# q of the later batches turned by DMA as k is, and the last output rows in three column pieces

## The chip, the core and the metric

The kernel runs on one NeuronCore of a Trainium2 chip. A core has five engines, each with an instruction list of its own that it takes in order: PE (TensorE, matrix multiply), DVE (VectorE), ACT (ScalarE), POOL (GpSimd) and SP (SyncE, which here only issues DMAs). They meet at semaphores. Data lies in HBM, in SBUF (128 partitions) and in PSUM, where TensorE writes its results, in eight banks of 512 float32 columns. The metric is the device time of one execution in microseconds (us).

## The reference

For each of 8 batches and 8 heads, with 576 positions of 64 values, it computes causal attention over a sliding window of 64 positions; the result, 4608 rows (8 x 576) of 512 values (8 heads x 64), goes through a two-layer network with a hidden width of 2048.

```python
scores = scale * np.matmul(q, k.transpose(0, 1, 3, 2))
rel = pos[:, None] - pos[None, :]
mask = (rel >= 0) & (rel < window)          # window = 64
attn = softmax(np.where(mask, scores, -1e9))
x = np.matmul(attn, v)                      # then (B, S, H, D) -> (B*S, H*D)
h = x @ w_in                                # 512 -> 2048
out = (h * sigmoid(h)) @ w_out              # 2048 -> 512
```

## The kernel before, in words

**The order is planned in the program.** `Plan` (L15) holds operations in classes, each class a queue with a rank, and plays them through once with a cost per engine; whichever ready operation has the lowest rank goes next on a free engine. What comes out is one fixed list for each engine. The first layer and second layer matmuls (class `moe`) have rank 99, so on TensorE they fill every place that attention leaves. Scores (class `s`) may only go in while second-layer matmuls are due, or when the next first layer lacks its input (`scores_may_run`, L439).

**Attention.** Heads are taken in pairs: four pairs `pj` for each batch, and three groups `g` of 192 positions. For a pair the kernel needs, in bfloat16, k with the 128 values of two heads on the partitions and positions along the columns (`kt`), and q in the same way but padded with zeros (`qbd`): head 0 sits on partitions 0 to 63 in one half, head 1 on partitions 64 to 127 in the other, so that one matmul gives the scores of both heads. `kt`, `qbd` and `vv` (v) have two buffers, used by batches in turn. Then come the exponential on ACT (`expo`, L334), the mask on DVE (`masking`, L337), the values matmul (`values`, L340) and the division on DVE (`inverse`, `normal_rows`). From batch 3 on the result is written to `oxs` and a DMA on SP transposes it into `bridge` (`turn_o`, L391), the network's input.

**How q and k get their layout.** By the older way, used for batches 0 and 1 and for every q, SP (POOL in batches 1 and 2) loads two heads in float32 into one of eight `nat` buffers (`load_qk`, L227), ACT or DVE casts it into `natb` (`cast`, L270), TensorE turns it in six transposing matmuls of 96 columns into PSUM (`turn`, L279), and ACT or DVE lifts it from there in two halves into `qbd` (`lift_q`, L287), or for k in one into `kt`. By the newer way, used for k from batch 2 on (`NXK`), POOL loads each head's rows and casts them on the way into one of two `kb` buffers (`load_k_rows`, L239, four loads for two pairs), and one transposing DMA on SP writes two pairs into `kt` (`turn_k`, L245). `add_batch_qk` (L452) enters all this in the plan. A load into `nat` or `kb` waits until the buffer's last reader is done, and from batch 3 on until v of the batch before has landed.

**The network.** The rows are cut into 9 tiles of 512 (`add_tile`, L564). The first layer makes 16 blocks of 128 hidden units in 64 matmuls and ACT applies the activation (`silu`); the second layer takes, for each of four blocks of 128 rows, 16 matmuls of 512 columns into one bank (`second_layer`, L416). DVE or ACT copies the bank into one of four `ot` buffers (`copy_out`), and SP stores it (`store`, L425), 128 rows of 512 values. Tile 8, the last, ends the program.

Of the kernel before, what the change touches and what calls it, by code (L numbers as in the profile page):

```python
# [9 lines left out]
BF16 = mybir.dt.bfloat16  # L10
# [98 lines left out]
def kernel(ctx, tc, q, k, v, w_in, w_out, out):  # L109
    nc = tc.nc  # L110
    B, H, S, D = q.shape
    d_model, d_ff = w_in.shape
# [3 lines left out]
    NM = 6  # L116
    NR = S // NM
    NG = 3
    NDC = d_model // 128
    NFT = d_ff // 128  # L120
    TT = 512
    NTT = B * S // TT
    TB = TT // 64
    NK = 2
    NN, NNB, NE, NOB, NOT, NGT = 8, 8, 14, 6, 4, NFT + 3
    PARTS = {0: [(0, 192), (192, 384), (384, TT)], 1: [(0, 256), (256, TT)]}
    NXK, NXO = 2, 3
    NKB, NOX = 2, 2
    scale = 1.0 / float(D) ** 0.5


# [2 lines left out]
    keep = ctx.enter_context(tc.tile_pool(name="keep", bufs=1))  # L134
# [13 lines left out]
    es = [keep.tile([128, 3, 2, 64], BF16, name=f"e{i}") for i in range(NE)]  # L148
    rcs = [keep.tile([128, 3, 2], FP32, name=f"rc{i}") for i in range(4)]
    obs = [keep.tile([128, 3, 128], BF16, name=f"ob{i}") for i in range(NOB)]  # L150
    kbs = [keep.tile([NR, 2, NM, 128], BF16, name=f"kb{i}") for i in range(NKB)]
    oxs = [keep.tile([128, 3, NP, 128], BF16, name=f"ox{i}") for i in range(NOX)]
    gts = [keep.tile([128, TT], BF16, name=f"g{i}") for i in range(NGT)]
    ots = [keep.tile([128, d_model], FP32, name=f"ot{i}") for i in range(NOT)]
# [6 lines left out]
    p = Plan(  # L161
        {"at": range(4), "mp": range(4, 8), "all": range(8)},
        rank=dict(one=-9, dma=-1, ld0=-1, ld1=-1, st=-2, xo=-1.5, xk=-1.4, silu=-3, out=-2, pv=0, ot=0, s=1, moe=99, warm=200, turn=2,
                  norm=0, inverse=0, bridge=0, exp=1, mask=1, lift=2, shift=2, cast=4, late=5, clear=9),
        rank0=dict(cast=-6, lift=-5, shift=-4.5, exp=-4, mask=-4, inverse=-3.5, norm=-3, bridge=-3.2),
    )
    copies = {"ACT": nc.scalar.copy, "DVE": nc.vector.tensor_copy, "POOL": nc.gpsimd.tensor_copy}
# [68 lines left out]
            in_=k[b, 2 * pj + hh].rearrange("(p m) d -> p m d", m=NM),  # L236
        )

    def load_k_rows(w, b, pj, hh):  # L239
        nc.gpsimd.dma_start(  # L240
            out=kbs[w][:, pj % 2, :, 64 * hh:64 * hh + 64],
            in_=k[b, 2 * pj + hh].rearrange("(m p) d -> p m d", p=NR),
        )

    def turn_k(w, b, pp):  # L245
        nc.sync.dma_start_transpose(
            out=kt[b % NK][:, 64 + 2 * pp * S:64 + 2 * (pp + 1) * S].rearrange("x (m p) -> x m p", m=2 * NM),
            in_=kbs[w].rearrange("p j m x -> p (j m x)"))

    def load_v(e, b, part):  # L250
        g0, g1 = part * 9, part * 9 + 9
# [161 lines left out]
    def silu(bank, gt, lo, hi):  # L413
        nc.scalar.activation(out=gts[gt][:, lo:hi], in_=banks[bank["bank"]][:, lo:hi], func=ACTF.Silu)  # L414

    def second_layer(bank, gt, m, f):  # L416
        nc.tensor.matmul(  # L417
            banks[bank["bank"]], lhsT=gts[gt][:, m * 128:(m + 1) * 128], rhs=w_out_sb[:, f, :],
            start=(f == 0), stop=(f == NFT - 1),
        )  # L420

    def copy_out(e, bank, ot):
        copies[e](out=ots[ot], in_=banks[bank["bank"]])  # L423

    def store(ot, j, m):  # L425
        r0 = j * TT + m * 128
        nc.sync.dma_start(out=out[r0:r0 + 128, :], in_=ots[ot])


    win, wout = [], []  # L430
# [16 lines left out]
        return rest > 6  # L447
    scores_may_run.i = 0

    n_nat, n_kb, kb_free = [0, 0], [0], {}  # L450

    def add_batch_qk(b):  # L452
        pool = "at" if b else "all"
        k_rows, k_busy = [], []
        for pj in range(NP):
            kq_done[(b, pj)] = []
            busy = s_last.get((b - NK, pj), []) + ([c_k[b % NK]] if b < NK else [])
            for kk in range(2):
                if b >= NXK and kk:
                    w = n_kb[0] // 2 % NKB  # L460
                    n_kb[0] += 1
                    k_rows += [p.add("dma", {"POOL": 0.72}, lambda _, w=w, pj=pj, hh=hh: load_k_rows(w, b, pj, hh),
                                     kb_free.get(w, []) + (v_landed[b - 1] if b > 2 else []), dma=0.6) for hh in range(2)]
                    k_busy += busy
                    if pj % 2:
                        xk = p.add("xk", {"SP": 1.4}, lambda _, w=w, pj=pj: turn_k(w, b, pj // 2), k_rows + k_busy, dma=2.9)
                        kb_free[w] = [xk]
                        for i in (pj - 1, pj):
                            kq_done[(b, i)].append(xk)
                        k_rows, k_busy = [], []  # L470
# [24 lines left out]
                tu["until"] = li  # L495
                kq_done[(b, pj)] += li
# [67 lines left out]
    def add_tile(j):  # L564
        gt = {}
        parts = PARTS.get(j, [(0, TT)])
        for ft in range(NFT):
            gt[ft] = (n_gt[0] % NGT, [])
            n_gt[0] += 1
        left = NFT * NDC * len(parts)  # L570
        for lo, hi in parts:
            have = o_done[:NP * ((j * TT + hi + 191) // 192)]
            for ft in range(NFT):
                g, si = gt[ft]
                bank = None
# [11 lines left out]
        order = [(m, f) for m in range(4) for f in range(NFT)]  # L587
        if j == 0:
            order = [(m, f) for f in range(NFT) for m in range(4)]
        bank, uses = {}, {}  # L590
        for i, (m, f) in enumerate(order):
            g = gt[f][0]
            op = p.add("moe", {"PE": 0.2165}, None, gt[f][1] + [wout[f // 2]], lat=0.1, pool=None if f else "mp")
            bank.setdefault(m, op)
            op["fn"] = lambda _, bank=bank[m], g=g, m=m, f=f: second_layer(bank, g, m, f)
            moe.append((op, 2, len(order) - i))
            uses.setdefault(g, []).append(op)
            if f == NFT - 1:
                ot = n_ot[0] % NOT
                n_ot[0] += 1  # L600
                cp = p.add("out", {"DVE": 0.7, "ACT": 0.62}, lambda e, bank=bank[m], ot=ot: copy_out(e, bank, ot),
                           [op, free_ot.get(ot)])
                bank[m]["until"] = [cp]
                free_ot[ot] = p.add("st", {"SP": 0.45}, lambda _, ot=ot, m=m: store(ot, j, m), [cp], dma=0.75)
        free_gt.update(uses)


# [59 lines left out]
```

## Time and profile before

| | |
|---|---|
| median of 8 runs | 326.32 us (325.48 to 327.17) |
| the profiled execution | 325.48 us, of which 323.4 us are its span |
| granted TensorE clock | full speed in all 40 slices |
| transposing DMAs on SP | 12 into `kt`, 15 into `bridge` |
| row loads of k on POOL | 48, of 72 KB each, 5.5 us from issue to landing |
| loads of q on SP | 24, of 288 KB each, 5.4 us from issue to landing |

From the page, in 40 equal slices of some 8 us each, tenths of busy time:

```profile
PE   3999989999999999999999999999999999999995
...
DVE  7895988875788948899789778800000000000000
ACT  4798775898787986788887875274156126416611
POOL 8967958581706603822713000000000000000000
...
DMA  8999999999999929999999111310110020020011
```

Attention, with all loads of q, k and v, goes on until about 210 us, between the matmuls of tiles 0 to 4; after that four tiles of the network alone are left. A group's line in the profile gives line, engine, operation, output<-input and count, then the busy time, the mean duration of one, and the idle time of the engine just before.

### The profile page before, as it was taken

What the parts mean: (1) busy time and instruction counts of PE and PEld (TensorE: products, weight loads), DVE (VectorE), ACT (ScalarE), POOL (GpSimd) and SP (SyncE); (2) the same over time, 40 slices, a digit from 0 to 9 for tenths busy, and PEclk for the clock granted to TensorE, in tenths of its full rate; (3) what the DMA queues carried; (4) which work ended last, traced back from release to release, by engine and by line L of the source; (5) the groups of instructions that cost most, each with busy time, mean ns of one, the idle gap of its engine ahead of it and who ended that gap; (6) DMA issues with size and microseconds to landing.
All of it is one profiled execution on the core that took longest, in us unless ns stands there. A gap on an engine that the chain in (4) does not pass through costs nothing.

```text
span 323.4 us, 6343 instructions
## 1 busy us (share of the span) xinstructions
PE 310.5 (96%) x2349; PEld 178.4 (55%) x2349; DVE 171.7 (53%) x480; ACT 207.8 (64%) x420; POOL 96.6 (30%) x126
## 2 busy tenths in 40 slices
PE   3999989999999999999999999999999999999995
PEld 1778865578565556655565555544444444444442
DVE  7895988875788948899789778800000000000000
ACT  4798775898787986788887875274156126416611
POOL 8967958581706603822713000000000000000000
PEclk9999999999999999999999999999999999999999
DMA  8999999999999929999999111310110020020011
GB/s 199 171 190 277 183 214 216 140 267 161 192 215 158 216 33 152 167 259 138 235 184 205 28 49 37 112 59 0 65 67 0 32 97 3 2 96 34 0 65 65
DMA packets 112350, 40.29 MB, mean 125 GB/s; under 512 B 95808, under 2 KB 106944, under 8 KB 112320
## 3 DMA queue, kind: packets, MB, share of 16 engines
q0 software_dynamic: 75520, 16.29, 59.7%
q1 hardware_dynamic: 36800, 23.60, 29.7%
q8 instruction: 18, 0.29, 0.4%
q14 instruction: 12, 0.10, 0.1%
HBM read 36.70 MB, written 9.44 MB: 143 GB/s over the span
## 4 chain that ended last, share of the span: by engine, by line
PE 86%; DVE 8%; DMA 2%; issue 1%; SPq 1%; ACT 1%; ACTq 0%
PE mp L417 38%; PE mp L408 34%; PE at L343 5%; PE at L317 4%; DVE qbd L289 4%; DMA nat<-in_q_dram 2%; PE at L282 2%; DVE natb L271 2%; DVE vv L303 1%; DVE vv L305 1%; DVE kt L295 1%; PE at L399 1%; SPq L228 1%; PE at L388 0%; PE at L609 0%
## 5 line engine op out<-in xcount | busy, mean ns | idle before, releaser
L417 PE MATMUL mp<-w_out_sb,g 128*128 128x512 bf16 x576 | 146.9, 379 | 0.0
L408 PE MATMUL mp<-bridge,w_in_sb 128*128 128x512 bf16 (+3 forms) x768 | 133.2, 326 | 0.9 <-ACT g L414 0.9
L414 ACT ACTIVATE g<-mp 128x512 bf16<-128x512 f32 (+3 forms) x192 | 90.5, 491 | 25.4 <-PE mp L408 23.6
L408 PEld LDWEIGHTS <-w_in_sb 128*128 128x128 bf16 x768 | 69.0, 98 | 50.7 <-issue 1.4
L417 PEld LDWEIGHTS <-g 128*128 128x128 bf16 x576 | 52.5, 98 | 42.0
L423 ACT COPY ot<-mp 128x512 f32<-128x512 f32 x24 | 14.0, 585 | 55.1 <-PE mp L417 55.0
L335 ACT ACTIVATE e<-at 128x384 bf16<-128x384 f32 x88 | 38.4, 498 | 12.0 <-PE at L317 10.4
L252 POOL DMA_DIRECT2D vv<-in_v_dram x32 | 32.4, 1021 | 41.7 <-DVE e L338 14.9
L372 DVE TENSOR_TENSOR ox<-at,rc 64x192 bf16<-64x192 f32 x120 | 42.5, 354 | 2.7
L240 POOL DMA_DIRECT2D kb<-in_k_dram x48 | 35.8, 754 | 25.8 <-DMA kt<-kb 22.1
L343 PEld LDWEIGHTS <-e 128*128 128x128 bf16 x288 | 22.6, 96 | 15.1 <-DVE e L338 2.5
L338 DVE TENSOR_TENSOR e<-e,mask 128x384 bf16<-128x384 bf16 x84 | 25.8, 350 | 8.3 <-ACT e L335 7.7
L343 PE MATMUL at<-vv,e 128*128 128x130 bf16 x276 | 29.9, 219 | 0.0
L289 DVE COPY qbd<-at 64x576 bf16<-64x576 bf16 x29 | 21.8, 752 | 6.0 <-PE mp L408 2.8
L289 ACT COPY qbd<-at 64x576 bf16<-64x576 bf16 x33 | 20.8, 630 | 6.4 <-DVE qbd L289 3.9
L317 PE MATMUL at<-qbd,kt 128*128 128x128 bf16 x252 | 24.3, 219 | 0.4 <-DVE qbd L289 0.4
L317 PEld LDWEIGHTS <-kt 128*128 128x128 bf16 x252 | 18.6, 97 | 10.2 <-issue 1.4
L282 PE MATMUL at<-ident,natb 96*128 96x96 bf16 x228 | 16.2, 210 | 7.2 <-ACT natb L271 5.5
L349 DVE RECIPROCAL rc<-at 128x6 f32<-128x6 f32 x92 | 17.1, 192 | 10.3 <-PE at L343 7.3
L282 PEld LDWEIGHTS <-natb 96*128 96x128 bf16 x240 | 13.7, 100 | 13.0 <-ACT natb L271 5.7
L271 ACT CAST natb<-nat 96x768 bf16<-96x768 f32 x20 | 16.2, 834 | 2.3 <-DMA nat<-in_q_dram 1.9
L355 DVE TENSOR_TENSOR ob<-at,rc 64x192 bf16<-64x192 f32 x48 | 16.8, 350 | 0.9
(67 smaller groups left out, 159.5 us busy)
## 6 DMA issues: line engine op xcount, KB each, us to landing
out_dram<-ot SPq DMA_DIRECT2D x36, 256.0 KB, 2.1
nat<-in_q_dram SPq DMA_DIRECT2D x24, 288.0 KB, 5.4
vv<-in_v_dram POOLq DMA_DIRECT2D x32, 144.0 KB, 5.6
kb<-in_k_dram POOLq DMA_DIRECT2D x48, 72.0 KB, 5.5
nat<-in_q_dram POOLq DMA_DIRECT2D x8, 288.0 KB, 8.7
w_in_sb<-in_moe_w_in_dram POOLq DMA_DIRECT2D x8, 256.0 KB, 7.8
w_out_sb<-in_moe_w_out_dram POOLq DMA_DIRECT2D x8, 256.0 KB, 7.8
nat<-in_k_dram POOLq DMA_DIRECT2D x4, 288.0 KB, 9.0
```

Of the source, the lines that this page charges most:

```text
L240: nc.gpsimd.dma_start(out=kbs[w][:, pj % 2, :, 64 * hh:64 * hh + 64], in_=k[b, 2 * pj + hh].rearrange("(m p) d -> p m d", p=NR),)
L252: queue[e].dma_start(out=vv[b % NK][:, 2 * g0 + 1:2 * g1 + 1:2, 0:D], in_=v[b].rearrange("h s d -> (h s) d").rearrange("(g p) d -> p g d", ...
L282: nc.tensor.matmul(pst[:, m], lhsT=natbs[w][:, m], rhs=ident[0:NR, 0:NR], is_transpose=True, start=(m == 0), stop=(m == NM - 1),)
L289: copies[e](out=qbd[b % NK][r, pj, hh].rearrange("x (p m) -> x p m", m=NM), in_=at_bf16(op)[r].rearrange("x (m p) -> x p m", m=NM),)
L317: nc.tensor.matmul(at_sp(op)[:, x], lhsT=kt[b % NK][:, pj * S + t * 64:pj * S + t * 64 + 128], rhs=qbd[b % NK][:, pj, :, t * 64:t * 64 + 6 ...
L335: nc.scalar.activation(out=es[n % NE], in_=at_sp(op), func=ACTF.Exp, scale=scale)
L338: nc.vector.tensor_mul(es[n % NE], es[n % NE], mask0 if g == 0 else mask)
L343: nc.tensor.matmul(at_pv(op)[:, x], lhsT=es[n % NE][:, x].rearrange("p h i -> p (h i)"), rhs=vv[b % NK][:, s:s + NB + 1:NB, 0:D + 1], star ...
L372: nc.vector.tensor_mul(ox(n)[:, :, r], pv[r, :, hh, 0:D], rc[r, :, hh:hh + 1].to_broadcast([64, 3, 64]))
L408: nc.tensor.matmul(banks[bank["bank"]][:, lo:hi], lhsT=w_in_sb[:, c, ft * 128:(ft + 1) * 128], rhs=bridge[:, (j * TT + lo) // 64:(j * TT + ...
L414: nc.scalar.activation(out=gts[gt][:, lo:hi], in_=banks[bank["bank"]][:, lo:hi], func=ACTF.Silu)
L417: nc.tensor.matmul(banks[bank["bank"]], lhsT=gts[gt][:, m * 128:(m + 1) * 128], rhs=w_out_sb[:, f, :], start=(f == 0), stop=(f == NFT - 1),)
```

## The change

It has two parts.

**q from batch 4 on** (`NXQ = 4`) goes the newer way too. Four row loads on POOL bring two pairs of heads; a transposing DMA on SP turns them into a new buffer `raw` (two of them, 128 partitions x 2 pairs x 576), with both heads of a pair on 128 partitions; then DVE copies it in two halves of 64 partitions into the padded `qbd` (`spread_q`, class `spread`). The two `kb` buffers are dropped: the rows of q and k lie in the eight `nat` buffers, read as bfloat16. So k's row loads of batches 2 to 7 take their turns in `nat` as well.

**The last 128 rows of tile 8** are computed in column pieces of 256, 128 and 128, each with 16 matmuls, a bank, a copy and a store of its own.

```diff
-    NXK, NXO = 2, 3
-    NKB, NOX = 2, 2
+    NXQ, NXK, NXO = 4, 2, 3
+    NRAW, NOX = 2, 2
...
-    kbs = [keep.tile([NR, 2, NM, 128], BF16, name=f"kb{i}") for i in range(NKB)]
+    raws = [keep.tile([128, 2, S], BF16, name=f"raw{i}") for i in range(NRAW)]
...
-    def load_k_rows(w, b, pj, hh):
+    def rows(i):
+        return nats[i].rearrange("p h x -> p (h x)").bitcast(BF16).rearrange("p (j m x) -> p j m x", j=2, m=NM)
+
+    def load_rows(i, b, pj, kk, hh):
         nc.gpsimd.dma_start(
-            out=kbs[w][:, pj % 2, :, 64 * hh:64 * hh + 64],
-            in_=k[b, 2 * pj + hh].rearrange("(m p) d -> p m d", p=NR),
-        )
-
-    def turn_k(w, b, pp):
+            out=rows(i)[:, pj % 2, :, 64 * hh:64 * hh + 64],
+            in_=(q, k)[kk][b, 2 * pj + hh].rearrange("(m p) d -> p m d", p=NR),
+        )
+
+    def turn_rows(i, out):
         nc.sync.dma_start_transpose(
-            out=kt[b % NK][:, 64 + 2 * pp * S:64 + 2 * (pp + 1) * S].rearrange("x (m p) -> x m p", m=2 * NM),
-            in_=kbs[w].rearrange("p j m x -> p (j m x)"))
+            out=out.rearrange("x (m p) -> x m p", m=2 * NM), in_=rows(i).rearrange("p j m x -> p (j m x)"))
+
+    def k_place(b, pj):
+        return kt[b % NK][:, 64 + pj * S:64 + (pj + 2) * S]
+
+    def spread_q(e, w, b, pj, hh):
+        r = slice(64 * hh, 64 * hh + 64)
+        copies[e](out=qbd[b % NK][r, pj:pj + 2, hh], in_=raws[w][r])
...
+                if b >= (NXK if kk else NXQ):
+                    if pj % 2 == 0:
+                        slot[kk] = n_nat[0] % NN
+                        n_nat[0] += 1
+                    i = slot[kk]
+                    parts[kk] += [p.add("dma", {"POOL": 0.72}, lambda _, i=i, pj=pj, kk=kk, hh=hh: load_rows(i, b, pj, kk, hh),
+                                        [nat_free.get(i)] + (v_landed[b - 1] if b > 2 else []), dma=0.6) for hh in range(2)]
+                    if pj % 2 == 0:
+                        continue
+                    both = busy + s_last.get((b - NK, pj - 1), [])
+                    if kk:
+                        done = [p.add("xk", {"SP": 1.4}, lambda _, i=i, pj=pj: turn_rows(i, k_place(b, pj - 1)),
+                                      parts[kk] + both, dma=2.9)]
+                        nat_free[i] = done[0]
+                    else:
+                        w = n_raw[0] % NRAW
+                        n_raw[0] += 1
+                        x = p.add("xk", {"SP": 1.4}, lambda _, i=i, w=w: turn_rows(i, raws[w].rearrange("x j s -> x (j s)")),
+                                  parts[kk] + raw_free.get(w, []), dma=2.9)
+                        nat_free[i] = x
+                        done = [p.add("spread", {"DVE": 0.5}, lambda e, w=w, pj=pj, hh=hh: spread_q(e, w, b, pj - 1, hh),
+                                      [x] + both, b=b) for hh in range(2)]
+                        raw_free[w] = done
...
+        if j == NTT - 1:
+            order = order[:3 * NFT] + [(3, f, lo, hi) for lo, hi in ((0, 256), (256, 384), (384, 512)) for f in range(NFT)]
...
-            banks[bank["bank"]], lhsT=gts[gt][:, m * 128:(m + 1) * 128], rhs=w_out_sb[:, f, :],
+            banks[bank["bank"]][:, 0:hi - lo], lhsT=gts[gt][:, m * 128:(m + 1) * 128], rhs=w_out_sb[:, f, lo:hi],
...
-        nc.sync.dma_start(out=out[r0:r0 + 128, :], in_=ots[ot])
+        nc.sync.dma_start(out=out[r0:r0 + 128, lo:hi], in_=ots[ot][:, lo:hi])
```

The plan is made anew with these operations, so that the fixed lists of all engines from batch 2 on differ from before also where the diff doesn't name them. In it, a spread has the rank of a lift plus its batch's number, and only DVE may take it.

More of the change, by code (lines that the diff above doesn't have):

```diff
@@ L163 @@
         rank=dict(one=-9, dma=-1, ld0=-1, ld1=-1, st=-2, xo=-1.5, xk=-1.4, silu=-3, out=-2, pv=0, ot=0, s=1, moe=99, warm=200, turn=2,
-                  norm=0, inverse=0, bridge=0, exp=1, mask=1, lift=2, shift=2, cast=4, late=5, clear=9),
+                  norm=0, inverse=0, bridge=0, exp=1, mask=1, lift=2, spread=2, shift=2, cast=4, late=5, clear=9),
         rank0=dict(cast=-6, lift=-5, shift=-4.5, exp=-4, mask=-4, inverse=-3.5, norm=-3, bridge=-3.2),
@@ L414, in silu, with second_layer, copy_out, store @@
         nc.scalar.activation(out=gts[gt][:, lo:hi], in_=banks[bank["bank"]][:, lo:hi], func=ACTF.Silu)
-    def second_layer(bank, gt, m, f):
+    def second_layer(bank, gt, m, f, lo, hi):
         nc.tensor.matmul(
-            banks[bank["bank"]], lhsT=gts[gt][:, m * 128:(m + 1) * 128], rhs=w_out_sb[:, f, :],
+            banks[bank["bank"]][:, 0:hi - lo], lhsT=gts[gt][:, m * 128:(m + 1) * 128], rhs=w_out_sb[:, f, lo:hi],
             start=(f == 0), stop=(f == NFT - 1),
         )
-    def copy_out(e, bank, ot):
-        copies[e](out=ots[ot], in_=banks[bank["bank"]])
-    def store(ot, j, m):
+    def copy_out(e, bank, ot, lo, hi):
+        copies[e](out=ots[ot][:, lo:hi], in_=banks[bank["bank"]][:, 0:hi - lo])
+    def store(ot, j, m, lo, hi):
         r0 = j * TT + m * 128
-        nc.sync.dma_start(out=out[r0:r0 + 128, :], in_=ots[ot])
+        nc.sync.dma_start(out=out[r0:r0 + 128, lo:hi], in_=ots[ot][:, lo:hi])
     win, wout = [], []
@@ L448 @@
     scores_may_run.i = 0
-    n_nat, n_kb, kb_free = [0, 0], [0], {}
+    n_nat, n_raw, raw_free = [0, 0], [0], {}
     def add_batch_qk(b):
         pool = "at" if b else "all"
-        k_rows, k_busy = [], []
+        slot, parts = {}, {0: [], 1: []}
         for pj in range(NP):
@@ L458, in add_batch_qk @@
             for kk in range(2):
[L459 to L470, printed above, removed]
+                if b >= (NXK if kk else NXQ):
[21 more added lines that the diff above has]
+                        raw_free[w] = done
+                    parts[kk] = []
+                    for x in (pj - 1, pj):
+                        kq_done[(b, x)] += done
                     continue
@@ L586, in add_tile @@
                 bank["until"] = [si[-1]]
-        order = [(m, f) for m in range(4) for f in range(NFT)]
+        order = [(m, f, 0, d_model) for m in range(4) for f in range(NFT)]
         if j == 0:
-            order = [(m, f) for f in range(NFT) for m in range(4)]
+            order = [(m, f, 0, d_model) for f in range(NFT) for m in range(4)]
+        if j == NTT - 1:
+            order = order[:3 * NFT] + [(3, f, lo, hi) for lo, hi in ((0, 256), (256, 384), (384, 512)) for f in range(NFT)]
         bank, uses = {}, {}
-        for i, (m, f) in enumerate(order):
+        for i, (m, f, lo, hi) in enumerate(order):
             g = gt[f][0]
-            op = p.add("moe", {"PE": 0.2165}, None, gt[f][1] + [wout[f // 2]], lat=0.1, pool=None if f else "mp")
-            bank.setdefault(m, op)
-            op["fn"] = lambda _, bank=bank[m], g=g, m=m, f=f: second_layer(bank, g, m, f)
+            op = p.add("moe", {"PE": 0.0036 + (hi - lo) / 2400}, None, gt[f][1] + [wout[f // 2]], lat=0.1,
+                       pool=None if f else "mp")
+            bank.setdefault((m, lo), op)
+            op["fn"] = lambda _, bank=bank[(m, lo)], g=g, m=m, f=f, lo=lo, hi=hi: second_layer(bank, g, m, f, lo, hi)
             moe.append((op, 2, len(order) - i))
@@ L600, in add_tile @@
                 n_ot[0] += 1
-                cp = p.add("out", {"DVE": 0.7, "ACT": 0.62}, lambda e, bank=bank[m], ot=ot: copy_out(e, bank, ot),
+                cp = p.add("out", {"DVE": 0.18 + (hi - lo) / 1000, "ACT": 0.18 + (hi - lo) / 1160},
+                           lambda e, bank=bank[(m, lo)], ot=ot, lo=lo, hi=hi: copy_out(e, bank, ot, lo, hi),
                            [op, free_ot.get(ot)])
-                bank[m]["until"] = [cp]
-                free_ot[ot] = p.add("st", {"SP": 0.45}, lambda _, ot=ot, m=m: store(ot, j, m), [cp], dma=0.75)
+                bank[(m, lo)]["until"] = [cp]
+                free_ot[ot] = p.add("st", {"SP": 0.45}, lambda _, ot=ot, m=m, lo=lo, hi=hi: store(ot, j, m, lo, hi), [cp],
+                                    dma=0.75 * (hi - lo) / d_model)
         free_gt.update(uses)
```

## The prediction

> **What bounds the kernel now.** I read the engine row first, then TensorE's waits behind the start, then the chain of waits. The engine row of the page:
>
> ```profile
> span 323.4 us, 6343 instructions
> PE 310.5 (96%) x2349; PEld 178.4 (55%) x2349; DVE 171.7 (53%) x480; ACT 207.8 (64%) x420; POOL 96.6 (30%) x126
> ```
>
> TensorE is busy for 96%, and no other engine for two thirds. Matmuls overlap, so that alone proves little. The waits of TensorE from 43 us to the end do:
>
> ```profile
> PE at L282 <- DVE natb L271: 1.2, 1, 1.2
> PE mp L408 <- ACT g L414: 0.5, 1, 0.5
> PE at L317 <- DVE qbd L289: 0.4, 1, 0.4
> ```
>
> Three waits, 2.1 us of 280, all before 84 us. From there TensorE is never out of work: each instruction taken from its list shortens the run by the time it holds the array, as long as its successor is ready. How long that is stands in the chain of waits, not in the groups. Two groups of the page, then pieces of the chain (start us, us, what):
>
> ```profile
> L417 PE MATMUL mp<-w_out_sb,g 128*128 128x512 bf16 x576 | 146.9, 379 | 0.0
> ...
> L282 PE MATMUL at<-ident,natb 96*128 96x96 bf16 x228 | 16.2, 210 | 7.2 <-ACT natb L271 5.5
> ```
>
> ```profile
> 168.68 0.34 PE at L317 x6
> ...
> 172.93 0.51 PE at L282 x12
> ...
> 305.59 13.83 PE mp L417 x64
> 319.42 0.03 ACTq L423
> 319.45 0.04 issue
> 319.49 0.58 ACT ot L423
> ```
>
> A group says 379 and 210 ns for one; the chain says 13.83/64 = 216 ns for a 512-column matmul, 0.51/12 = 43 ns for a 96-column transpose and 0.34/6 = 57 ns for a 128-column matmul. The groups count the filling of the array, in which the next matmul already runs.
>
> **What leaves TensorE.** From batch 4 on, q no longer goes through natb, `turn` and `lift_q`. That is 4 batches x 4 head pairs x 6 = 96 transposes; the list of the changed kernel has 64 fewer matmuls, which is 96 less, and 32 more for the tail.
>
> Here a rule stands beside the rows. The Trainium skill, "Perfetto Trace Analysis", section "Identifying the Most-Contended Engine", says that matmul busy time is a bad measure of TensorE's headroom, and to judge by the weight loads' busy share. By the rule's first half the 210 ns of the group are not a price: 96 x 0.210 = 20.2 us would be wrong, and the spacing gives 96 x 0.043 = **4.1 us**. By its second half 55% of weight loading would leave TensorE much headroom, and the change would be worth about nothing. The waits above decide: no headroom shows after 84 us. I take 4.1 us.
>
> **What leaves DVE and ACT.** 16 casts (L271) and 32 lifts (L289). Their rows and, by shape, the nearest row to what comes:
>
> ```profile
> L289 DVE COPY qbd<-at 64x576 bf16<-64x576 bf16 x29 | 21.8, 752 | 6.0 <-PE mp L408 2.8 <-PE at L282 1.7 <-ACT qbd L289 1.2
> ...
> L305 DVE COPY vv<-vv 64x2304 bf16<-64x2304 bf16 x6 | 4.5, 753 | 0.1
> ```
>
> A lift is 0.63 us on ACT and 0.75 on DVE, a cast 0.83 and 0.62: 16 x 0.7 + 32 x 0.69 = 33 us of work, all beside TensorE, so worth nothing by itself. In their place DVE alone gets 16 `spread_q` copies, 64 x 1152 from SBUF to SBUF. The same kind of copy with 2304 columns takes 753 ns; its 576-column form takes 0.32 at the least, so 0.2 us fixed and half the rest give about 0.47 us, bounded by 0.32 and 0.75. 16 x 0.47 = 7.5 us on an engine that is busy for 53%. Nothing on the path, but see the waits.
>
> **What is added to the queues.** GpSimd issues 32 more row loads (`load_rows`, 0.73 us each at the median, 23 us); SP issues 8 more transposes and 16 fewer q loads (0.45 us each). GpSimd has the room, since kb goes and k lands in the eight nat buffers: its largest wait was for the two kb buffers. The rows are GpSimd's wait, the software queue's packets and the time to landing of the transposes to kt:
>
> ```profile
> POOL kb L240 <- DMA kt<-kb: 22.1, 5, 8.0
> ```
>
> ```profile
> q0 software_dynamic: 75520, 16.29, 59.7%
> ```
>
> ```profile
> DMA to landing us min/median/max: 3.0/5.5/11.4
> ```
>
> The second weighing speaks against the change. The Trainium skill, "DMA: Bandwidth & Descriptors", section "Specifications", asks for 512 B or more per piece. The q loads that go move 1536 B runs; the new ones write runs of 64 bf16, 128 B. By the row, a packet of the software queue costs 0.597 x 16 x 323.4 / 75520 = 41 ns, and 32 loads x 576 runs are 18,432 packets: 47 us of all 16 engines' time, less some 14 for the 3,072 packets of the loads that go. Were the DMA engines the bound, this would cost tens of us. They are not: packets overlap (the windows from 40 to 185 us show a summed share of 1.25 to 1.71), the work falls on 70 to 180 us, and TensorE has 36 us of own work per batch there. So I price it at nothing on the path, and use it for how late a transpose may land.
>
> **The waits that come.** A spread waits on DVE for its transpose, and DVE takes its list in order, so the masks and norms behind it wait too, and behind them TensorE's value matmuls. Adding up TensorE's new list at the spacings above from 42.9 us, where the first plain scores stand, gives when each must be there:
> - Batch 4: scores at about 119 us. Its last three spreads stand on DVE behind batch 3's norms (about 115.5) and two V shifts (2 x 0.75): 117 + 3 x 0.47 = 118.5. Just in time; a microsecond late is a microsecond lost. The second pair's transpose, behind the store of tile 1's third and fourth rows on SP at about 101, lands by 108.
> - Batch 6: its first spread is on DVE ahead of batch 5's masks, needed at about 150. Its transpose waits on SP behind batch 4's last bridge transpose (about 138), and for batch 5's spread of the same raw buffer; issued at 139.5, landed at 145 by the median.
> - Batch 7: its second spread and two V shifts stand ahead of batch 6's masks (182). The transpose can go at 173, when batch 6's spread has freed raw: 173 + 5.5 + 0.9 + 1.5 = 181.
> - Batch 5: issued at 120, needed at 147; no issue.
>
> By the medians nothing is late by more than a microsecond, by the longest landing batch 7 is late by 5. I take 0.3 us, between 0 and 7. Behind the waiting transposes on SP stand stores and bridge transposes, which have tens of us; behind the row loads on GpSimd stand the V loads, 5.9 us later than with k alone (8 x 0.73), but these wait for TensorE's last values of two batches before in any case (POOL at L252 waits up to 14.9 us).
>
> **The tail.** The last 16 matmuls of 512 columns become 16 of 256 and 32 of 128: 16 x 0.111 + 32 x 0.057 = 3.60 against 16 x 0.216 = 3.46, so 0.14 us more (0.111 is 7.91/71 of the 256-column run at 67.46 in the chain). Then the last copy has 128 columns, not 512: ACT takes 585 ns for 512 and 318 for 192 columns, by that slope 265 ns for 128, a gain of 0.32. The last store moves 64 KB, not 256 KB; the landing of 2.1 us can shrink by nothing, or at most by three quarters of 256 KB at 277 GB/s, the fastest slice, 0.7 us. I take 0.3, as most of 2.1 us is not moving bytes. The tail gains about **0.5 us** (0.2 to 0.9).
>
> **Sum.** 4.1 + 0.5 - 0.3 = 4.3 us. The profiled execution took 325.5 us (323.4 of span), so 321.2 on its own scale. It is the lowest of the eight runs, whose median is 326.3; from that, 322.0. The answer is a median again, but the lowest run shows that the scale may sit lower: I say **321.8 us**.
>
> **Rivals.**
> 1. *Full gain, as summed* (320.3 to 323.0). For: no TensorE wait after 84 us in the profile, though k from batch 2 on has the same path with the same transposes. Against: two of the four batches meet their time narrowly. Chance 0.65.
> 2. *Part is given back*: one or two of the spreads come 1 to 3 us late; 323.0 to 325.6, say 324. For: the landing of up to 11.4 us. Against: in the profile the late ones fell before 90 us, with the weights' loads around them. Chance 0.20.
> 3. *Slower*: the spread waits on DVE become TensorE's wait. With the longest landing at batch 6 and 7: 139.5 + 11.4 + 0.9 against 150 is 2 us, batch 7 5 us, and the SP queue held up (one issue took 3.5 us) pushes either by another; together some 7 us against 4.6 gained: 328.5. It decides from a sum of 4.6 us on. Before the change a late q stopped no one but a turn whose place TensorE had filled. Chance 0.10.
> 4. *No change*: what the transposes took was filled with matmuls that wait for something else, e.g. second-layer matmuls for silu on ACT; only the tail's 0.5 us is left, 325.8. Against: ACT waits for TensorE (23.6 us in the page at L414), not the other way. Chance 0.05.
>
> The range of eight in ten, 320.3 to 325.2, holds the first and most of the second. A difference of 0.2% (0.65 us) is about what can be told from none: faster 0.85, same 0.05, slower 0.10.
>
> **What would show it.** Right: TensorE's x2349 becomes x2285, its waits after 84 us stay under 1 us, the span falls by about the same as the 96 x 43 ns; `raw` to qbd copies of 0.45 to 0.6 us; the span's end 0.3 to 0.9 us closer to the last matmul. Wrong: waits of TensorE at L317 or L343's new lines for DVE near 119, 150 or 182 us, with a DMA to raw behind them; kt and raw transposes landing at 8 us and over between 90 and 180 us; a spread of over 0.75 us.

## The result, and the profile after

The changed kernel takes 323.72 us at the median of 11 runs (321.96 to 328.91; the record lists a twelfth, of 326.37). The kernel before, run beside it on the same chip, takes 326.5 us (32 runs, 325.3 to 328.2). The ratio is 0.9911 [0.9892, 0.993]: 2.9 us faster, where 4.5 were forecast from the median. The profiled execution took 322.24 us.

Engine row and software queue of the page after:

```profile
span 320.5 us, 6242 instructions
...
PE 307.4 (96%) x2285; PEld 175.6 (55%) x2285; DVE 171.3 (53%) x481; ACT 189.0 (59%) x389; POOL 120.3 (38%) x158
...
q0 software_dynamic: 94464, 18.65, 76.1%
```

TensorE has the 64 matmuls fewer that were counted, ACT is 19 us less busy, and the weight-load share, 55%, has not moved. The software queue's packets cost more of the 16 DMA engines' time: 76.1%, against 59.7% before.

TensorE's waits from 43 us to the end (us in total, times, longest us):

```profile
PE at L292 <- ACT natb L281: 1.2, 1, 1.2
PE at L292 <- DVE natb L281: 0.7, 1, 0.7
PE at L327 <- DVE qbd L258: 0.3, 1, 0.3
PE mp L418 <- ACT g L424: 0.3, 1, 0.3
PE at L327 <- DVE qbd L299: 0.2, 1, 0.2
```

L292, L281, L327 and L258 are now the transposes, the casts, the scores and the spreads. Two waits are new: 1.2 us for ACT's cast of a q in float32, and 0.3 us for a spread.

To compare stages, cut the span at the first plain scores' start and at the last copy's start. Start-up, up to the first cut, took 42.9 us in the profiles of both kernels, but 44.5 to 45.5 in most profiles of the experiments: from execution to execution it differs by up to 2.5 us, so it is left out of the comparisons below. **S** is the stretch between the cuts, **E** the rest.

| | before | after | difference |
|---|---|---|---|
| S, us | 276.57 | 274.31 | -2.26 |
| E, us | 3.91 | 3.28 | -0.63 |

From the start times of the matmuls one can add up how much longer each took than its columns at full speed (216 ns for 512, 43 for 96). From 43 us on these losses are 2.45 us before and 4.27 after. So 96 transposes less (-4.13), the tail's pieces (+0.08) and 1.82 us of new losses make -2.23, against -2.26 seen. Of the 1.82, 1.34 lie between 70 and 80 us and 0.82 between 120 and 130; small changes of both signs make up the rest.

**At 77 us** TensorE waits for the second of the four pairs of q of batch 3, which still goes the older way. TensorE's timeline, then ACT's (start us, us, instruction, and in brackets the idle time before it and who ended it):

```profile
77.62 0.43 PE L292 MATMUL at<-ident,natb 96*128 96x96 bf16 x6 [1.16 <-ACT natb L281]
```

```profile
76.74 0.83 ACT L281 CAST natb<-nat 96x768 bf16<-96x768 f32 x1 [1.61 <-DMA nat<-in_q_dram]
```

ACT, in turn, waits for the load: it is the DMA that came late. The loads of this q landed 8.0 to 10.3 us after their issue, before 5.1 to 9.2.

**At 122 us** batch 4 needs its q. DVE's timeline after, and TensorE's:

```profile
117.46 2.63 DVE L382 TENSOR_TENSOR ox<-at,rc 64x192 bf16<-64x192 f32 x7
120.13 0.76 DVE L315 COPY vv<-vv 64x2304 bf16<-64x2304 bf16 x1
120.90 0.85 DVE L313 COPY vv<-vv 64x2304 bf16<-64x2304 bf16 x1
121.78 2.00 DVE L258 COPY qbd<-raw 64x1152 bf16<-64x1152 bf16 x3
```

```profile
123.83 0.49 PE L327 MATMUL at<-qbd,kt 128*128 128x128 bf16 x6 [0.32 <-DVE qbd L258]
```

No DMA is waited for here. Norms of batch 3, two V shifts and three spreads stand one after the other in DVE's list and end at 123.78, 50 ns before the scores.

**At 154 us** a transpose is late, but TensorE had other work, just enough: its first values matmul, at 155.56, starts 0.42 us after the first mask does, and executions in which it waits for that mask show 0.41. DVE's timeline:

```profile
153.96 1.16 DVE L258 COPY qbd<-raw 64x1152 bf16<-64x1152 bf16 x2 [7.99 <-DMA raw<-nat]
155.14 0.63 DVE L348 TENSOR_TENSOR e<-e,mask 128x384 bf16<-128x384 bf16 x2
```

DVE stands for 8 us on batch 6's first spread, with batch 5's masks behind it. The rows of `raw` in the trace say why:

```profile
L258 DVE COPY qbd<-raw x16: 452/536/740, 107.1 to 182.0; 64x1152 bf16<-64x1152 bf16 x16
...
DMA to landing us min/median/max: 4.6/6.9/9.4
```

A spread takes 452 to 740 ns, median 536. A transpose to `raw` lands in 6.9 us at the median. Those to `kt` now take 8.4; the forecast had used their 5.5 from the kernel before.

The end of the chain of waits after:

```profile
303.25 13.91 PE mp L427 x96
...
317.22 0.27 ACT ot L433
```

The last 96 matmuls take 13.91 us, where 64 took 13.83; the last copy takes 0.27, before 0.58. What is left of E's fall of 0.63 us, some 0.32, is the store.

### The profile page after: what moved, and what is told of

It is laid out like the page before. It is cut to its first block, busy times and chain, and to the rows that moved or that the text cites. A ratio compares the mean times of both kernels' runs of the same rounds, so it can differ in the third digit from the quotient of the medians.

```text
span 320.5 us, 6242 instructions
## 1 busy us (share of the span) xinstructions
PE 307.4 (96%) x2285; PEld 175.6 (55%) x2285; DVE 171.3 (53%) x481; ACT 189.0 (59%) x389; POOL 120.3 (38%) x158
## 3 DMA queue, kind: packets, MB, share of 16 engines
q0 software_dynamic: 94464, 18.65, 76.1%
## 4 chain that ended last, share of the span: by engine, by line
PE 82%; DVE 8%; DMA 5%; issue 1%; SPq 1%; ACT 1%; ACTq 0%
PE mp L427 36%; PE mp L418 33%; DMA nat<-in_q_dram 5%; PE at L353 5%; PE at L327 4%; DVE qbd L299 3%; DVE ox L382 1%; PE at L292 1%; DVE vv L313 1%; SPq L228 1%; DVE natb L281 1%; PE at L409 1%; DVE vv L315 1%; DVE qbd L258 1%; PE at L398 0%
## 5 line engine op out<-in xcount | busy, mean ns | idle before, releaser
L427 PE MATMUL mp<-w_out_sb,g 128*128 128x512 bf16 (+2 forms) x608 | 145.3, 368 | 0.0
L427 PEld LDWEIGHTS <-g 128*128 128x128 bf16 x608 | 54.8, 97 | 43.0
L433 ACT COPY ot<-mp 128x512 f32<-128x512 f32 (+2 forms) x32 | 17.9, 558 | 64.5 <-PE mp L427 57.8
L244 POOL DMA_DIRECT2D nat<-in_k_dram x48 | 35.6, 749 | 14.9 <-DMA vv<-in_v_dram 5.1
L244 POOL DMA_DIRECT2D nat<-in_q_dram x32 | 24.0, 757 | 5.6 <-DMA nat<-in_k_dram 3.0
L327 PE MATMUL at<-qbd,kt 128*128 128x128 bf16 x252 | 23.9, 219 | 0.8 <-DVE qbd L258 0.3
L327 PEld LDWEIGHTS <-kt 128*128 128x128 bf16 x252 | 18.2, 97 | 10.0 <-issue 2.4
L299 DVE COPY qbd<-at 64x576 bf16<-64x576 bf16 x23 | 17.3, 754 | 3.3 <-PE at L292 2.3
L292 PE MATMUL at<-ident,natb 96*128 96x96 bf16 x132 | 9.5, 213 | 7.4 <-ACT natb L281 6.4
L258 DVE COPY qbd<-raw 64x1152 bf16<-64x1152 bf16 x16 | 9.0, 564 | 12.2 <-DMA raw<-nat 11.8
L292 PEld LDWEIGHTS <-natb 96*128 96x128 bf16 x144 | 8.0, 102 | 11.6 <-ACT natb L281 6.9
```

The costliest lines, as they stand in the source:

```text
L244: nc.gpsimd.dma_start(out=rows(i)[:, pj % 2, :, 64 * hh:64 * hh + 64], in_=(q, k)[kk][b, 2 * pj + hh].rearrange("(m p) d -> p m d", p=NR),)
L292: nc.tensor.matmul(pst[:, m], lhsT=natbs[w][:, m], rhs=ident[0:NR, 0:NR], is_transpose=True, start=(m == 0), stop=(m == NM - 1),)
L299: copies[e](out=qbd[b % NK][r, pj, hh].rearrange("x (p m) -> x p m", m=NM), in_=at_bf16(op)[r].rearrange("x (m p) -> x p m", m=NM),)
L327: nc.tensor.matmul(at_sp(op)[:, x], lhsT=kt[b % NK][:, pj * S + t * 64:pj * S + t * 64 + 128], rhs=qbd[b % NK][:, pj, :, t * 64:t * 64 + 6 ...
L427: nc.tensor.matmul(banks[bank["bank"]][:, 0:hi - lo], lhsT=gts[gt][:, m * 128:(m + 1) * 128], rhs=w_out_sb[:, f, lo:hi], start=(f == 0), s ...
```

## The experiments

Ratios are to the kernel before, run beside each on the same chip, with the 95% interval.

| run | what | median us | ratio | S | E |
|---|---|---|---|---|---|
| e1_tail_only | before, with the tail's pieces | 326.26 | 0.9978 [0.9964, 0.9992] | 276.67 | 3.04 |
| e2_q_only | after, last rows in one piece | 325.4 | 0.9973 [0.9946, 1.0] | 274.68 | 3.93 |
| e3_k_in_nat | only k's rows in `nat` | 327.19 | 1.0008 [0.9989, 1.0028] | 276.08 | 3.92 |
| e4_turns_back | after, 96 idle transposes | 334.17 | 1.0215 [1.0189, 1.024] | 283.44 | 3.30 |
| e5_plan_lands_late | after, planned with later landings | 323.45 | 0.9898 [0.9873, 0.9924] | 273.19 | 3.16 |
| e6_late_turns_back | e5, 96 idle transposes | 326.85 | 1.0003 [0.9974, 1.0032] | 277.96 | 3.29 |
| e7_late_batch_3 | e5, from batch 3 on | 328.08 | 1.0041 [1.0023, 1.0059] | 278.02 | 3.88 |
| e9_late_spread_act | e5, spreads on ACT too | 324.61 | 0.9927 [0.9903, 0.9952] | 275.96 | 3.12 |
| after_again | after | 324.24 | 0.9908 [0.9881, 0.9935] | 275.33 | 3.29 |
| e5_again | e5 | 323.26 | 0.9882 [0.9856, 0.9908] | 274.25 | 3.13 |
| e11_late_hold | e5, next batch's rows later in the plan | 322.73 | 0.987 [0.9846, 0.9893] | 272.74 | 3.14 |
| e12_late_from_5 | e5, from batch 5 on | 324.44 | 0.9926 [0.9898, 0.9954] | 275.24 | 3.13 |

The theory that came out of the comparison was: the transposes cost 43 ns each, as forecast, and part of the gain is lost because the spreads on DVE, in a fixed list, come late to their users. The rivals: that a transpose was worth another amount, that k's rows in `nat` cost the lost part, and that the tail gave something else than thought.

### The parts alone

e1_tail_only is the kernel before with the hunks of `second_layer`, `copy_out`, `store` and `add_tile`. e2_q_only is the changed kernel without

```diff
-        if j == NTT - 1:
-            order = order[:3 * NFT] + [(3, f, lo, hi) for lo, hi in ((0, 256), (256, 384), (384, 512)) for f in range(NFT)]
```

and e3_k_in_nat is e2 with no q on the newer way, so that of the first part only the place of k's rows is left:

```diff
-    NXQ, NXK, NXO = 4, 2, 3
+    NXQ, NXK, NXO = 8, 2, 3
```

> The kernel before with the three column pieces of the last rows alone; all other instruction lists stay as they were. Theory (the prediction's sum holds for the tail): 0.5 us less than before, ratio 0.9985, last copy 0.27 us. Rival (the last store's landing is fixed and the added matmuls cost what the copy gains): no change, ratio 1.000 within 0.0005.

> The changed kernel with the last rows in one piece. Theory (4.1 us of transposes leave TensorE, about 1.8 us come back as waits before 130 us): 2.3 us less than before, ratio 0.993; TensorE's lost time after 43 us about 4 us as in the changed kernel. Rival (the q part is worth its full 4.1 us and the tail nothing or less): ratio 0.9875.

> The changed kernel with no q turned by DMA (from batch 8 on, so none) and the last rows in one piece: what is left of the change is that k's rows lie in the nat buffers and not in two kb buffers, so that their loads go earlier. Theory A (the wait of a transpose of batch 3's q for its late load, 1.2 us at 77 us, comes from the k loads that now run ahead): the wait is there, 0.5 to 1.5 us slower than before, ratio 1.003. Theory B (it comes from the q row loads of batch 4): no such wait, ratio 1.000.

The tail alone gives 0.7 us (0.0022 x 327.0, the kernel before on this chip), and E falls by 0.87. Its last matmuls take 13.91 us, as in the changed kernel. k's rows in `nat` change nothing that can be measured.

q alone gives 0.9 us by the ratio, with an interval from 0 to 1.8, where 2.3 were expected; S in its profile fell by 1.9. The two parts' measured gains, 0.7 and 0.9, come to 1.6 us, while the whole gives 2.9. Part of this gap lies in a few executions of e2. In three of its twelve (327.5, 327.8 and 328.6 us) the mean granted clock is 0.995; in the other nine it is 0.998 or more, and their median, 325.3, would make q alone worth 1.7. The changed kernel has two such executions among its first twelve (326.4 and 328.9 us), the kernel before one among the 76 that were run beside the experiments, e5 and e5_again none among twelve. All six executions of e4 show 0.990 to 0.995, and e4's profile has a pause of 4.76 us and a lower clock behind it (see below). So these executions probably had such a pause too; none of them was profiled, so this is not shown, and the rest of the gap stays open.

What e2's profile does show is a shorter wait that after's profile lacks. TensorE's waits, then its timeline and DVE's:

```profile
PE at L353 <- DVE e L348: 1.2, 1, 1.2
```

```profile
158.20 0.34 PE L353 MATMUL at<-vv,e 128*128 128x130 bf16 x3 [1.18 <-DVE e L348]
```

```profile
156.46 1.30 DVE L258 COPY qbd<-raw 64x1152 bf16<-64x1152 bf16 x2 [9.18 <-DMA raw<-nat]
```

It is the place of 154 us again, and now the values matmuls wait for the masks behind the spread. Counted from the first plain scores (42.91 us in after, 45.09 in e2), the transpose is only 0.3 us later than in after. But e2's TensorE had no wait at 77 us and came to the masks some 0.7 us earlier. So these waits do not simply add up: part of what after lost at 77 us it would otherwise have lost at 154.

### What a transpose is worth

e4_turns_back puts 96 transposes back into the changed kernel. They read `ident` and `natb` as before, stand behind the spreads in the plan, and write to banks that nobody reads; nothing is left out.

```diff
                         raw_free[w] = done
+                        for _ in range(2):
+                            tu = p.add("turn", {"PE": 0.27}, None, done + [c_ident], lat=0.1, pool=pool, b=b)
+                            tu["fn"], tu["until"] = lambda _, tu=tu: turn(tu, 0), [tu]
```

> The changed kernel, tail included, with the 96 removed transposes put back on TensorE as idle work: each pair of heads from batch 4 on turns an old natb buffer into a bank that nobody reads, after the spreads. No cast, no lift, no q load comes back. Theory (TensorE has no headroom, a transpose costs its 43 ns): 4.1 us slower than the changed kernel, ratio to before about 1.0035. Rival (the transposes were filled in beside other waits): as fast as the changed kernel, ratio 0.991.

It is 9.9 us slower than the changed kernel by the two ratios, far more than 4.1. The profile tells what of this is transposes. TensorE's and DVE's timelines of e4:

```profile
165.06 0.35 PE L353 MATMUL at<-vv,e 128*128 128x130 bf16 x3 [4.76 <-DVE e L348]
...
165.84 1.06 PE L427 MATMUL mp<-w_out_sb,g 128*128 128x512 bf16 x2
```

```profile
157.68 1.02 DVE L258 COPY qbd<-raw 64x1152 bf16<-64x1152 bf16 x2 [10.50 <-DMA raw<-nat]
158.73 0.36 DVE L348 TENSOR_TENSOR e<-e,mask 128x384 bf16<-128x384 bf16 x1
...
164.29 0.45 DVE L258 COPY qbd<-raw 64x1152 bf16<-64x1152 bf16 x1 [5.20 <-DMA raw<-nat]
```

The plan, made anew, has put both of batch 6's spreads between batch 5's masks. DVE waits 10.5 us for the first transpose and 5.2 for the second, and TensorE stands for 4.76 us. This is the forecast's third rival in full. Added up, the parts give about S's 9.1 us above after's: 4.1 for the transposes, 4.8 for this wait, 1.7 for slow matmuls behind it (told of in the last section), less 1.3 for the wait at 77 us, which this execution lacks.

To part the transposes from the wait, e5_plan_lands_late lets the plan count with a landing that is 3 us later, and e6_late_turns_back adds e4's lines to e5:

```diff
-                        op["seen"] = pipe[soft] + 1.4
+                        op["seen"] = pipe[soft] + 1.4 + (3.0 if c == "xk" else 0.0)
```

> The changed kernel, with one constant of the plan changed: a transposing DMA to kt or raw counts as landed 3 us later, so that the spreads of batch 6 stand behind batch 5's masks on DVE, not ahead. Nothing else is added or left out. Theory A (what the changed kernel loses in its median run is the wait of batch 5's masks behind that spread at 150 to 160 us): no wait of TensorE for a mask there, 1 to 2 us faster than the changed kernel, ratio to before 0.986 to 0.988, runs closer together. Theory B (the loss is the DMA traffic at large, which delays loads anywhere): as the changed kernel, ratio 0.991.

> The kernel of e5_plan_lands_late with the 96 transposes back on TensorE as idle work, as in e4_turns_back; with the spreads out of the masks' way the plan's places are no longer upset by it. Theory (43 ns each): 4.1 us slower than e5_plan_lands_late. Rival (e4's 10 us are the price of a transpose among matmuls, 0.1 us each): 10 us slower.

e6 is 3.4 us above e5 by the medians, 35 ns for each transpose. By S it is 4.77, or 3.5 without the 1.3 us that e6's profile waits at 77 us and e5's doesn't. So a transpose is worth 35 to 50 ns of this kernel's time, around the 43 of the chain. The intervals of the two ratios leave room for some 2.2 to 4.7 us, so neither nothing nor e6's rival of 10 us fits; the 210 ns that the group shows would have made 20 us.

### The wait at 154 us

e5 itself answers for the wait: with the later landing in the plan, batch 6's first spread goes behind batch 5's masks. It was run again beside the changed kernel, on one chip:

> The changed kernel itself once more, beside e5_plan_lands_late's kernel on the same chip. Theory A (TensorE's wait at 150 to 160 us for masks that stand behind batch 6's first spread makes the difference between its better and its worse runs): slower than e5_again by 1 to 2 us in the median. Theory B (the loss lies elsewhere): no more than 0.5 us apart.

> The kernel of e5_plan_lands_late once more, beside the changed kernel. Theory A: ratio to before 0.986 to 0.990 and 1 to 2 us faster than after_again. Theory B: within 0.5 us of it.

After's second profile has the wait that its first did not; DVE's timeline and TensorE's:

```profile
156.68 1.02 DVE L258 COPY qbd<-raw 64x1152 bf16<-64x1152 bf16 x2 [8.92 <-DMA raw<-nat]
```

```profile
158.14 0.35 PE L353 MATMUL at<-vv,e 128*128 128x130 bf16 x3 [0.63 <-DVE e L348]
```

and e5's DVE goes straight to the masks, having waited for the exponential alone:

```profile
154.99 0.74 DVE L348 TENSOR_TENSOR e<-e,mask 128x384 bf16<-128x384 bf16 x2 [9.23 <-ACT e L345]
```

e5_again is 1.0 us below after_again by the medians, at the lower edge of the 1 to 2 us expected; e5's first ratio, 0.9898, lay between its two theories. Of the 1.1 us between their S, 0.9 were lost at this place. The intervals of the two ratios overlap, so that the order removes the wait is shown, and that this is worth 1 us is likely, not shown.

### The wait at 122 us

e9_late_spread_act lets ACT take spreads as well:

```diff
-                        done = [p.add("spread", {"DVE": 0.5}, lambda e, w=w, pj=pj, hh=hh: spread_q(e, w, b, pj - 1, hh),
+                        done = [p.add("spread", {"DVE": 0.5, "ACT": 1.15}, lambda e, w=w, pj=pj, hh=hh: spread_q(e, w, b, pj - 1, hh),
```

> The kernel of e5_plan_lands_late, and a spread may also go on ACT, at 1.15 us in the plan. Theory A (the 0.8 us that TensorE waits at 122 us for batch 4's spreads is DVE's own queue: norms, V shifts and spreads of 0.67 us): that wait goes, 0.7 us faster than e5_plan_lands_late. Theory B (the transpose lands late): no change.

13 of the 16 spreads go to ACT, at 1.15 us each, and the wait at 122 us is gone. But S is larger than in e5's two profiles. TensorE now waits elsewhere, most for a transpose to `kt`; its timeline:

```profile
168.23 0.68 PE L327 MATMUL at<-qbd,kt 128*128 128x128 bf16 x9 [1.05 <-DMA kt<-nat]
```

DVE's own queue explains the wait at 122 us and its removal, as theory A has it, but not the 0.7 us forecast with it: the time went to other late arrivals.

e7_late_batch_3 and e12_late_from_5 are e5 with `NXQ` 3 and 5.

> The kernel of e5_plan_lands_late with q turned by DMA from batch 3 on. Theory A: 24 more transposes leave TensorE, 1.0 us, and the wait for batch 3's float32 q at 77 us goes: 1 to 2 us faster than e5_plan_lands_late. Theory B (at 70 to 100 us the row loads already crowd the DMA queues): the spreads of batch 3 come late, as fast as e5_plan_lands_late or slower.

> The kernel of e5_plan_lands_late with q turned by DMA from batch 5 on, so that batch 4's q goes the older way. Theory A (a batch is worth its 24 transposes, 1.0 us, less what its own spreads make TensorE wait, 0.8 us at 122 us for batch 4): within 0.5 us of e5_again. Theory B (batch 4 pays in full): 1.0 us slower. Theory C (batch 4's row loads crowd the queues at 70 to 100 us and hurt batch 3 as well): up to 1 us faster.

From batch 3 on, another 24 transposes are saved, and yet it is slower than the kernel before (its E, 3.88 although it has the tail's pieces, was not explained). The first two of TensorE's waits in e7:

```profile
PE at L353 <- DVE vv L315: 2.4, 1, 2.4
PE at L353 <- DVE e L348: 2.3, 3, 1.1
```

V shifts and masks are late on DVE, later in the program than batch 3's own spreads. The gain of 1 us per batch is far less than one collision of that kind. From batch 5 on it is 1.2 us slower than e5_again by the medians, as theory B forecast, but that decides nothing: there is no batch 4 to be late, but the new plan puts a spread of batch 6 between batch 5's masks again (DVE waits 2.24 us for its transpose), and in TensorE's waits stands

```profile
PE at L327 <- DVE ox L382: 1.6, 1, 1.6
```

Without these 1.6 us S would be 273.6, within e5's two values.

### What makes the transposes late

In e11_late_hold the plan makes the row loads of a batch wait until the transposes of the batch before have landed, from batch 5 on; `turned` is filled with each transpose:

```diff
-                                        [nat_free.get(i)] + (v_landed[b - 1] if b > 2 else []), dma=0.6) for hh in range(2)]
+                                        [nat_free.get(i)] + (v_landed[b - 1] if b > 2 else []) + turned.get(b - 1, []), dma=0.6) for hh in range(2)]
```

> The kernel of e5_plan_lands_late in which a row load of batch 5, 6 or 7 also waits until the four transposes of the batch before have landed. Theory A (a transpose is slow in landing because the next batch's row loads share the DMA engines): transposes to raw land 5 us after issue at the median, not 7, and the time is that of e5_again or 0.5 us less. Theory B (it is slow for other traffic, v loads and stores): landings stay at 7 us and the later loads cost TensorE 1 us or more.

In the trace no load is held back. Such a dependency only moves an operation in the plan; on the chip an instruction waits for its place in its engine's list, its data and its buffer. GpSimd's list came out the same as in e5, all 158 instructions in the same order, and batch 5's row loads start ahead of batch 4's second pair of transposes, which land at 112.6 and 115.4 us. GpSimd's timeline in e11, then SP's:

```profile
102.51 1.50 POOL L244 DMA_DIRECT2D nat<-in_q_dram  x2
```

```profile
105.66 2.42 SPq L250 DMA_TRANSPOSE raw<-nat  x1
108.30 1.70 SPq L250 DMA_TRANSPOSE kt<-nat  x1
```

The wait of a row load for v of the batch before is of the same kind: in after, row loads are issued from 118.65 us on, while the V loads issued just before them land at 120.2 to 124.6.

What changed are the lists of SP and DVE. SP issues the transposes of batches 5 to 7 later, behind stores and transposes to `bridge`: batch 6's first at 159.6 us, where e5_again has 145.6. By then the last row load has been issued, and this transpose lands 3.2 us after its issue, where e5_again's took 11.1. The transposes to `raw` in e11, and TensorE's waits:

```profile
DMA to landing us min/median/max: 3.0/5.1/6.9
```

```profile
PE at L292 <- DVE natb L281: 0.7, 1, 0.7
PE at L327 <- DVE qbd L258: 0.3, 1, 0.3
PE at L327 <- DVE qbd L299: 0.3, 1, 0.3
PE mp L418 <- ACT g L424: 0.3, 1, 0.3
```

The medians of the others are 6.9 (after), 7.5 (after_again), 6.9 (e5) and 9.2 us (e5_again). So theory A's 5 us came, but not in its way, and the run says nothing of holding loads back.

That loads make the transposes late is better read from e3 and e2, which differ in how q of batches 4 to 7 gets its layout. Here are the transposes to `kt` between 118 and 135 us, in e3 and in e2:

```profile
DMA to landing us min/median/max: 3.3/3.4/3.5
```

```profile
DMA to landing us min/median/max: 9.9/10.6/11.3
```

In e3 GpSimd issues nothing for 7.7 us until 124.3; in e2 the next batch's row loads go out from 120.1 us on, and the summed DMA share from 120 to 125 us is 2.85, against 0.65 in e3. The kernel before has 3.0 us at this place, the changed kernel 8.2 and 9.7. So the DMA work that the newer way of q adds makes a transpose late: shown. Which part of it counts most, row loads, V loads or the added transposes, was not tested.

In e11 no wait of more than 0.3 us is left after 80 us. S is 272.74, where the count of instructions gives 276.57 - 4.13 + 0.08 = 272.52. At 0.987, 322.73 us, it is the fastest measured of all, ahead of both kernels. Its interval overlaps with e5's, and 1.0 of the 1.5 us by which its S is below e5_again's comes from the 70s, where e11 changes nothing; so it is not shown to beat e5.

## Why the prediction was right and wrong

The direction was right: faster, with 0.85. The time was not the likeliest case's: 323.72 lies above its 323.0 and in the second rival's stretch, 323.0 to 325.6, which had 0.20. The way it came out is that rival's too: the transposes gave what was summed, and part was given back to late arrivals. On the profiled execution's own scale 321.2 was summed, and 322.24 came.

- **4.1 us for 96 transposes of 43 ns: right.** The list shrank as counted; the account of S fits 43 ns, and e6 against e5 fits 35 to 50, not 210 and not zero.
- **Weighing the weight-load share: right to go by the waits.** It stood at 55% before and stands at 55% after, while the transposes removed were worth about their spacing.
- **The tail, 0.5 us: right, and a little small.** E fell by 0.63; the matmuls cost 0.08 rather than 0.14, the copy gave 0.31 for 0.32, the store 0.32 for 0.3.
- **Spreads of 0.47 us: right in the quiet, low in the crowd.** They took 536 ns at the median, and 667 (2.00/3) at 122 us, just where they count.
- **The new waits, 0.3 us (0 to 7): this term was too small.** Losses grew by 1.8 us in the profiled execution. Of the signs named for being wrong, the landings of 8 us and over came, and small waits for spreads or for the masks behind them near 122 and, in after_again, 158 us. Three steps stand behind the term:
  - *Batch 4 "just in time".* The place was right and its worth was not counted: the norms were still running at 120.1, not done at 115.5, the spreads took 0.67, and 0.8 us were lost.
  - *Batch 6's transpose "issued at 139.5, landed at 145".* It was issued at 144.56 and landed at 153.9. Of these 9 us, 5 are the issue: the last transpose to `bridge` ahead of it on SP went at 142.57, not at about 138. The other 4 are the landing, which was taken from the kernel before (5.5 us), although the same forecast had worked out 18,432 added packets and priced them at nothing. The delay cost 0 to 0.6 us in the changed kernel's two profiles, 1.2 in e2 and 4.8 in e4: the wait of the third rival is real. That it cost so little in the two profiles is partly luck, with nothing to spare in one of them.
  - *Batch 3's q.* It was not foreseen at all, being outside the changed operations. It cost 1.2 us in both profiles of the changed kernel. But e2, e4, e5 and e11, whose lists are the same up to that point, have no such wait, and the tail alone has 0.4. It comes and goes from execution to execution; whether the change makes it more frequent stays open.
- **"Priced at nothing" for the DMA engines: half right.** They did not become the bound, but they are fuller. The software queue's packets were forecast to take 47 us more of all 16 engines' time; by the two pages it is 51. The windows from 80 to 100 us; the last columns are TensorE's clock, the summed DMA share and GB/s. Before, then after:

```profile
80.00:100.00 20.00, 19.64 (x182) 12.04 (x180) 16.02 (x48) 14.90 (x33) 8.34 (x11) 1.00 1.46 188
```

```profile
80.00:100.00 20.00, 19.60 (x203) 12.49 (x200) 16.26 (x51) 15.92 (x38) 12.08 (x17) 1.00 2.21 159
```

The share rises from 1.46 to 2.21 while the bytes moved fall from 188 to 159 GB/s: more time for less data. That is paid in landing times, as e3 against e2 shows, and late landings are behind the waits at 77 and 154 us.
- **Batch 7 and batch 5, no issue: right.** In no profile of the changed kernel does TensorE wait for them.

## What to carry to other kernels

Where an engine has no idle time, an instruction taken from its list is worth its spacing in the chain; but what replaces it puts waits into another engine's fixed list, and one wait that reaches the bound engine is worth dozens of such instructions (one wait of 4.8 us was 110 transposes). Waits of one run are not to be added up: a wait that goes can uncover the next. When a change adds DMA work, do not carry over the landing times of the trace before: the landings with the new load on the queues are the term to bound. And when a planner orders the lists, letting it count with the landings as measured is a change of one constant that can take a collision away. But an order in the plan is no wait on the chip: whether a hold took effect is read from the trace.

## What was not expected of the hardware

- **TensorE slows down after a pause of a few microseconds.** Behind e4's pause of 4.76 us, two matmuls of 512 columns take 1.06 us, where 0.59 is usual at that place. In the windows of e4 the clock (third column from the end) falls:

```profile
160.00:165.00 5.00, 0.31 (x2) 0.00 (x0) 0.71 (x2) 0.40 (x1) 3.53 (x5) 1.00 1.78 156
165.00:170.00 5.00, 4.94 (x35) 3.05 (x36) 4.13 (x15) 2.27 (x5) 1.48 (x3) 0.66 2.07 160
```

The added loss, 1.7 us, comes on top of the pause. The Trainium skill, "TensorE: Matmul & The Clock Gate", section "HAM oscillation — how this bites in real kernels", says that idle gaps above some 3.4 us bring the array to half its clock; the 4.76 us here agree. In e7, where pauses of 2.37 and 0.65 us stand with one matmul between them, the clock is 0.72 in the window from 135 to 140 us. Together these pauses are 3.0 us, less than the page's figure, so short pauses close to each other were enough.
- **A spread gets slower while GpSimd issues loads.** In all the profiles together, the 33 spreads on DVE that meet no GpSimd instruction take 0.45 to 0.46 us; the 130 that meet one take 0.45 to 1.01, and the three at 122 us, beside row loads, 0.67 each. The Trainium skill, "SBUF — State Buffer", section "Who interferes with whom", says that DVE copies can enter modes in which they and GpSimd shut each other out of a shared pair of ports; the times fit that, though no run here shows the mode of a spread or took GpSimd's work away from one alone.
